# A gated mix of linear attention and an MLP block: column sums moved from TensorE to VectorE, a mask built on GpSimd, and the first loads re-ordered

## The chip, the cores and the metric

The kernel runs on one core of a Trainium2 chip. The metric is device time in microseconds (us), from fourteen runs of the program; beside it stands one execution taken with the profiler. All times below are us from the start of that execution's span unless marked ns. TensorE (PE) multiplies matrices, VectorE (DVE) and ScalarE (ACT) do elementwise work, GpSimd (POOL) does small arithmetic and masks, and SyncE (SP) issues most transfers. Each engine runs its own instructions in order and waits on semaphores for the others.

## The reference

The input x has 2048 rows (tokens) and 640 columns. The output is g * a + (1 - g) * b with a gate g per token.

```
g  = sigmoid((x * gate_w).sum(-1))
# a: linear attention, 32 heads of 20
q, k, v = x @ wqkv                      # 3 x [2048, 640]
phi(t)  = where(t > 0, t + 1, exp(t)) + 1e-6
kv  = sum_s phi(k)[s, d] * v[s, e]      # per head, 20 x 20
z   = sum_s phi(k)[s, d]                # per head, 20: column sums over all tokens
o   = (phi(q) @ kv) / (phi(q) @ z + 1e-6)
a   = o @ wo
# b: mixer block
h   = gelu(layernorm(x) @ w1);  hs = four column groups of h shifted by 1, -1, 2, -2 tokens
x1  = x + hs @ w2
b   = x1 + gelu(layernorm(x1) @ w3) @ w4
```

## The kernel before, in words

Tokens are cut into 16 chunks of 128 (index c), columns into 5 blocks of 128 (index dc). The whole program is written out by hand in one order per engine; PSUM is four buffers of 128 x 1024 float32 that `alloc` and `release` pass round in turn. A matmul needs its contraction along partitions, so x is held twice: as it is (`x_sb`) and transposed (`xT`).

*Start (lines 159 to 342).* Weights of K and the first three x chunks are loaded. Five matmuls on zeros (L308) keep TensorE busy until they arrive. TensorE turns chunks 0 to 2 itself (`x_tr`, L320), and VectorE and ScalarE copy the result out of PSUM (L321, L322). All later chunks of `xT` come by transposing DMAs (L157) that `late_loads` issues on SyncE, with the plain x loads (L154) in between, and then all further weights. A memset of one column of xT (L327), which VectorE does after the copy of chunk 0, holds that list back: the first transposing DMA writes over the same column and has to wait for it. GpSimd builds `mask4`, a 0/1 matrix of which columns belong to which head. TensorE transposes it (L313) and ScalarE copies the result to `E4` (L314), the expansion matrix which spreads a value per head over 4 partitions.

*K stage (L345).* For each chunk: ten matmuls (L252) make k in PSUM; ScalarE takes exp (L244), VectorE makes phi from it (L247, L248) and stores it in `pk`. A G step (L261) follows: x.T @ phi(k), accumulated over chunks.

*Q stage (L383).* Ten Q tiles of 128 x 1024 (L390), each followed by five or six G steps, and by its own phi on ScalarE and VectorE. In between, VectorE does LayerNorm (`ln1_apply`, L226), whose result SyncE transposes by DMA into `lnxT` (L228). After the third tile `z_rows` (L359) sums phi(k) over all tokens on TensorE: 32 matmuls against a matrix of ones (L364), the four chunks of a group in the four column strips, so that each sum comes out 32 times over. ScalarE copies it (L366), VectorE splits it into two bf16 parts (L368, L369). After the fifth tile `z_cols` (L371) adds the strips and turns the sums into columns by ten one-column matmuls (L376, L377) against 1/32; VectorE makes `Zb`, the sums masked by head (L378, L381).

*W1 stage (L495).* A `w1_unit` is ten matmuls (L423), then gelu on ScalarE (L428, L431). Between these units stand the small steps of attention: `den_unit` (the denominators, L470), `rec_piece` (their reciprocals in four pieces, L477), `kv_unit` (L443), six `m_unit`s (L457, the product of kv and wo), `m_move` (through DRAM and back, L462), `rexp_unit` (E4 spreads the reciprocals, L484) and `scale_q` (L493). The order of these calls is the order on each engine. SyncE's loads of W3 (L514) and W4 (L527 to L530) come after `m_move` in the same queue.

*The rest.* W2 (L556) with the residual add (L558) and second LayerNorm, then W3 (L571), the attention output (L597), W4 (L638) and the stores (L609).

Of the kernel before, what the change touches and what calls it, by code (L numbers as in the profile page):

```python
# [8 lines left out]
ACT = mybir.ActivationFunctionType  # L9
# [7 lines left out]
def kernel(  # L17
# [14 lines left out]
    P = 128  # L32
# [20 lines left out]
    def sb(name, cols, dt=BF16):  # L53
        return const.tile([P, cols], dt, name=name)
# [46 lines left out]
    kvT = sb("kvT", 6 * GW)[:].rearrange("p (g d) -> p g d", g=6)  # L101
    warm = sb("warm", 512)
    ident = sb("ident", P)
    ones32 = sb("ones32", 32)
    c32 = sb("c32", 1)
    mask4 = sb("mask4", P)
    mask32 = mask4[:, 0:32]
    E4 = sb("E4", P)
    bmask = sb("bmask", GW, F32)
    g5 = sb("g5", P)  # L110
# [26 lines left out]
    def alloc():  # L137
        return free.pop(0)

    def release(i):  # L140
        free.append(i)
# [11 lines left out]
    def load_x(c0, c1):  # L153
        sp.dma_start(x_sb[:, c0:c1, :], xv[:, c0:c1, :])  # L154

    def load_xT(c0, c1):
        sp.dma_start_transpose(xT[:, :, c0 * P:c1 * P], x2[c0 * P:c1 * P, :])  # L157
# [8 lines left out]
    for dc in range(3):  # L166
# [4 lines left out]
    sp.dma_start(wkg[:, 3:5, 0:D], A_wqkv[3 * P:5 * P, D:2 * D].rearrange("(j p) d -> p j d", p=P))  # L171


    nc.gpsimd.memset(mask4[:], 1.0)
    m4 = mask4[:].rearrange("p (f h) -> p f h", f=4)
    nc.gpsimd.affine_select(out=m4, in_=m4, compare_op=ALU.is_ge, fill=0.0, base=0,
                            pattern=[[0, 4], [-4, 32]], channel_multiplier=1)
    nc.gpsimd.affine_select(out=m4, in_=m4, compare_op=ALU.is_ge, fill=0.0, base=3,
                            pattern=[[0, 4], [4, 32]], channel_multiplier=-1)
    for dc in range(DC):  # L180
        nc.gpsimd.memset(wkg[:, dc, D + 1:D + 2], 1.0)
    nc.gpsimd.memset(ones32[:], 1.0)
    nc.gpsimd.memset(c32[:], 1.0 / 32)
    nc.gpsimd.memset(nhalf[:], -0.5)
    nc.gpsimd.memset(bmask[:], 1.0)
    bm3 = bmask[:].rearrange("p (h e) -> p h e", e=DH)
# [1 line left out]
                            pattern=[[-DH, 6], [0, DH]], channel_multiplier=1)  # L188
    nc.gpsimd.affine_select(out=bm3, in_=bm3, compare_op=ALU.is_ge, fill=0.0, base=DH - 1,
                            pattern=[[DH, 6], [0, DH]], channel_multiplier=-1)  # L190
    nc.gpsimd.memset(hsT[:, :, 0:4], 0.0)
    nc.gpsimd.memset(hsT[:, :, S:S + 4], 0.0)

# [39 lines left out]
    def pop(q, n=1):  # L233
        for _ in range(n):
            if q:
                q.pop(0)()
# [13 lines left out]
    def k_mm(c, p, dc):  # L250
        for (n0, n1) in ((0, 512), (512, KW)):
            mm(PP[p][:, n0:n1], lhsT=xT[:, dc, c * P:(c + 1) * P], rhs=wkg[:, dc, n0:n1],  # L252
               start=(dc == 0), stop=(dc == DC - 1))
# [21 lines left out]
            g_post(i, gp[0])  # L275

    def late_loads():
        load_xT(3, 4)
        load_xT(4, 5)
        load_x(3, 4)  # L280
        load_xT(5, 6)
        load_xT(6, 7)
        load_x(4, 6)
        load_xT(7, 8)
        load_xT(8, 10)
        load_x(6, 9)
        load_xT(10, 11)
        load_xT(11, 13)
        load_x(9, 12)
        load_xT(13, 16)  # L290
        load_x(12, 16)
        rows = lambda w, a, b: w[:, a:b].rearrange("(j p) d -> p j d", p=P)
        sp.dma_start(wq, rows(A_wqkv, 0, D))
        sp.dma_start(w1, rows(B_w1, 0, D))
        sp.dma_start(wv, rows(A_wqkv, 2 * D, 3 * D))
        sp.dma_start(wo6[0:GW, 0:5, :], A_wo[0:5 * GW, :].rearrange("(g r) d -> r g d", r=GW))
        sp.dma_start(wo6[0:gsz[5], 5, :], A_wo[5 * GW:D, :])
        sp.dma_start(w2[:, 0:4, :], B_w2.rearrange("(g c) d -> c g d", c=CG)[0:P])
        for g in range(4):
            sp.dma_start(w2[32 * g:32 * (g + 1), 4, :], B_w2[CG * g + P:CG * (g + 1), :])  # L300
        w1g = w1.rearrange("p k (g c) -> p k g c", c=CG)
        w1x4 = w1x.rearrange("p k (g c) -> p k g c", g=4)
        for g in range(4):
            nc.gpsimd.tensor_copy(w1x4[:, :, g, :], w1g[:, :, g, P:CG])


    for _ in range(5):
        mm(PP[3][:, 512:1024], lhsT=warm[:, 0:P], rhs=warm[:], start=True, stop=True)  # L308
    tg = PP[0][:, 512:1024].bitcast(BF16)
    nc.tensor.transpose(tg[:, 0:DC], g5[0:DC, :], ident[0:DC, 0:DC])  # L310
    for dc in range(DC):
        nc.vector.tensor_copy(wkg[:, dc, D:D + 1], tg[:, dc:dc + 1])
    nc.tensor.transpose(PP[1][:, 0:64].bitcast(BF16), mask4[:], ident[:])  # L313
    act(E4[:], PP[1][:, 0:64].bitcast(BF16), ACT.Copy)  # L314

    def x_tr(c, a, b):
        ta, tb = PP[a][:, 0:512].bitcast(BF16), PP[b][:, 0:512].bitcast(BF16)
        for dc in range(DC):
            t, k = (ta, dc) if dc < 3 else (tb, dc - 3)
            nc.tensor.transpose(t[:, k * P:(k + 1) * P], x_sb[:, c, dc * P:(dc + 1) * P], ident[:])  # L320
        nc.vector.tensor_copy(xT[:, 0:3, c * P:(c + 1) * P], ta[:, 0:3 * P].rearrange("p (j s) -> p j s", j=3))  # L321
        act(xT[:, 3:5, c * P:(c + 1) * P], tb[:, 0:2 * P].rearrange("p (j s) -> p j s", j=2), ACT.Copy)  # L322
# [1 line left out]
    for _ in range(3):  # L324
        alloc()
    x_tr(0, 3, 2)
    nc.vector.memset(xT[:, 0, 3 * P:3 * P + 1], 0.0)  # L327
    late_loads()
    x_tr(1, 1, 2)
    k_mm(0, 0, 0)  # L330
    k_mm(0, 0, 1)
    x_tr(2, 3, 2)
    k_mm(1, 1, 0)
    k_mm(1, 1, 1)
    k_mm(2, 2, 0)
    k_mm(2, 2, 1)
# [19 lines left out]
    gq = [(0, c) for c in range(NCH - 3, NCH)] + [(i, c) for i in range(1, DC) for c in range(NCH)]  # L356
    wqp = wq.rearrange("p k (q j) -> p k j q", j=DC)

    def z_rows():  # L359
        p = alloc()  # L360
        for (n0, n1) in COLS:
            for cc in range(0, NCH, 4):
                for q in range(4):
                    mm(PP[p][32 * q:32 * (q + 1), n0:n1], lhsT=ones32[:], rhs=pk[:, cc + q, n0:n1],  # L364
                       start=(cc == 0), stop=(cc == NCH - 4), tile_position=(0, 32 * q), skip_group_check=True)
        act(zsb[:], PP[p][:, 0:D], ACT.Copy)  # L366
        release(p)
        nc.vector.tensor_copy(zhi[:], zsb[:])  # L368
        nc.vector.tensor_tensor(zlo[:], zsb[:], zhi[:], op=ALU.subtract)  # L369

    def z_cols():  # L371
        p = alloc()
        zh = zhi[:].rearrange("p (q j) -> p j q", j=DC)
        zl = zlo[:].rearrange("p (q j) -> p j q", j=DC)
        for j in range(DC):
            mm(PP[p][:, j:j + 1], lhsT=zh[:, j], rhs=c32[:], start=True, stop=False)  # L376
            mm(PP[p][:, j:j + 1], lhsT=zl[:, j], rhs=c32[:], start=False, stop=True)  # L377
        nc.vector.tensor_copy(zT[:], PP[p][:, 0:DC])  # L378
        release(p)
        for j in range(DC):  # L380
            nc.vector.tensor_scalar(Zb[:, j, :], mask32, zT[:, j:j + 1], None, op0=ALU.mult)  # L381

    n_ = 0  # L383
    for half in range(2):
        for j in range(DC):
            p = alloc()
            for dc in range(DC):
                for tt in range(2):
                    t0 = half * 1024 + tt * 512
                    mm(PP[p][:, tt * 512:(tt + 1) * 512], lhsT=wqp[:, dc, j], rhs=xT[:, dc, t0:t0 + 512],  # L390
                       start=(dc == 0), stop=(dc == DC - 1))
            phi(pqT[:, j, half * 1024:(half + 1) * 1024], PP[p][:], 1024)
            release(p)
            pop(ln1_s)
            if n_ in (1, 2, 3, 4, 7, 8):
                pop(ln1_a, 2)
            for _ in range(6 if n_ == 0 else 5):
                g_unit(*gq.pop(0))
            if n_ == 2:
                z_rows()  # L400
            if n_ == 4:
                z_cols()
            n_ += 1
    while gq:
        g_unit(*gq.pop(0))
    assert not ln1_s
    pop(ln1_a, 4)
    assert not ln1_a

# [56 lines left out]
    def den_unit():  # L466
        p = alloc()
        for j in range(DC):
            for t in range(4):
                mm(PP[p][32 * t:32 * (t + 1), 0:512], lhsT=Zb[:, j, :], rhs=pqT[:, j, t * 512:(t + 1) * 512],  # L470
                   start=(j == 0), stop=(j == DC - 1), tile_position=(0, 32 * t), skip_group_check=True)
        nc.vector.tensor_scalar(den[:], PP[p][:, 0:512], 1e-6, None, op0=ALU.add)
        release(p)

    def rec_piece(k):
        with nc.allow_low_precision(reason="bf16 operand of a product"):
            nc.vector.reciprocal(rden[:, k * P:(k + 1) * P], den[:, k * P:(k + 1) * P])  # L477
# [15 lines left out]
        nc.vector.tensor_tensor(pqT[:, j, s_], pqT[:, j, s_], rexp[:, s_], op=ALU.mult)  # L493

    w1_unit(0, 4)  # L495
    den_unit()
    rec_piece(0)
    w1_unit(0, 0)
    kv_unit()
    rec_piece(1)  # L500
    w1_unit(0, 1)
    m_unit(0)
    m_unit(1)
    rec_piece(2)
    w1_unit(0, 2)
    m_unit(2)
    m_unit(3)
    rec_piece(3)
    w1_unit(0, 3)
    m_unit(4)  # L510
    m_unit(5)
    m_move()
    for dc in range(DC):
        sp.dma_start(w3[:, dc, :], B_w3[dc * P:(dc + 1) * P, :])  # L514
    w1_unit(1, 4)
    w1_unit(1, 0)
    rexp_unit()
    w1_unit(1, 1)
    scale_q(0, 0)
    scale_q(1, 0)  # L520
    scale_q(2, 0)
    w1_unit(1, 2)
    scale_q(3, 0)
    scale_q(4, 0)
    w1_unit(1, 3)
    w4v = B_w4[0:NF * P, :].rearrange("(f p) d -> p f d", p=P)
    sp.dma_start(w4[0:FT, NF, :], B_w4[NF * P:F, :])  # L527
    sp.dma_start(w4[FT:2 * FT, NF, :], B_w4[NF * P:F, :])
# [159 lines left out]
```

## Time and profile before

| what | us |
|---|---|
| median of 14 runs (lowest to highest) | 267.26 (266.93 to 267.86) |
| the profiled execution: its time / its span | 267.64 / 265.9 |
| TensorE busy | 261.6 (98% of the span) |
| VectorE / ScalarE / GpSimd busy | 116.0 / 110.7 / 32.1 |
| K stage from the first turned chunk to the first Q tile | 3.7 to 31.9 |
| Q stage, W1 stage, W2 stage begin at | 31.9, 73.4, 100.1 |

TensorE's busy share is an upper figure, since matmuls are pipelined and their ends are modelled. The chain of work that ended last tells which engine each moment of the span hung on. A bracket at the end of a timeline row is the idle time of that engine before the instruction, and what ended it. Idle time of an engine that nobody waits for costs nothing.

### The profile page before, as it was taken

The numbers are of one execution on the slowest core, as the hardware profiler recorded it, in microseconds if no ns is written. First come the engines' busy times: TensorE is split into PE (matmuls) and PEld (weight loads), VectorE is DVE, ScalarE is ACT, GpSimd is POOL, SyncE is SP. The second block draws the span as 40 slices with busy tenths as digits, with TensorE's granted clock in tenths as the row PEclk, the third lists the DMA queues.
The fourth block names the chain that finished last, engine by engine and source line by source line (L and its number), as shares of the span: only waits on it lengthen the run. The fifth ranks groups of instructions, "written<-read, shape, count | busy, mean of one in ns | idle before, by whom it ended". The sixth has DMA issues, their size and how long they took to land.

```text
span 265.9 us, 4225 instructions
## 1 busy us (share of the span) xinstructions
PE 261.6 (98%) x1698; PEld 136.2 (51%) x1698; DVE 116.0 (44%) x212; ACT 110.7 (42%) x165; POOL 32.1 (12%) x110
## 2 busy tenths in 40 slices
PE   8999999999999999999999999999999999999995
PEld 4555555555545445554444455555544444555552
DVE  2487747665665165999920033233200002233232
ACT  3466664565355671234977522022034444022020
POOL 3000052020200000536770000000000000000000
PEclk9999999999999999999999999999999999999999
DMA  6799995431440269932752001001000000001001
GB/s 213 160 188 248 368 234 123 54 74 25 84 91 0 67 220 357 306 81 49 101 100 49 0 2 49 27 25 49 27 25 0 0 2 0 25 27 49 27 25 49
DMA packets 42207, 23.95 MB, mean 90 GB/s; under 512 B 31052, under 2 KB 41420, under 8 KB 42188
## 3 DMA queue, kind: packets, MB, share of 16 engines
q1 hardware_dynamic: 41602, 23.16, 36.1%
q10 hardware_dynamic: 586, 0.53, 0.6%
q8 instruction: 13, 0.21, 0.3%
q14 instruction: 6, 0.05, 0.1%
HBM read 12.86 MB, written 3.44 MB: 61 GB/s over the span
## 4 chain that ended last, share of the span: by engine, by line
PE 98%; DVE 1%; ACT 0%; issue 0%
PE pp L638 20%; PE pp L571 19%; PE pp L252 8%; PE pp L423 8%; PE pp L597 8%; PE pp L390 8%; PE pp L556 8%; PE pp L261 8%; PE pp L580 2%; PE pp L623 1%; PE pp L632 1%; PE pp L587 1%; PE pp L308 1%; PE pp L457 1%; PE pp L443 1%; PE pp L320 1%
## 5 line engine op out<-in xcount | busy, mean ns | idle before, releaser
L638 PE MATMUL pp<-RB,RXH 128*128 128x512 bf16 (+1 forms) x390 | 54.4, 299 | 0.0
L571 PE MATMUL pp<-lnxT,RA 128*128 128x512 bf16 x240 | 52.1, 379 | 0.0
L638 PEld LDWEIGHTS <-RXH 128*128 128x128 bf16 x390 | 29.7, 98 | 24.2 <-issue 2.1
L571 PEld LDWEIGHTS <-RA 128*128 128x128 bf16 x240 | 23.4, 98 | 28.1
L600 ACT ACTIVATE RXH<-pp,g_all 128x640 f32<-128x640 f32 x16 | 12.7, 794 | 54.9 <-PE pp L597 54.9
L573 ACT ACTIVATE RXH<-pp 128x1024 bf16<-128x1024 f32 x24 | 24.3, 1020 | 26.7 <-PE pp L571 26.7
L244 ACT ACTIVATE eb<-pp 128x640 bf16<-128x640 f32 (+1 forms) x26 | 21.4, 828 | 25.3 <-PE pp L390 16.3
L261 PE MATMUL pp<-RPK,RXH 128*128 128x512 bf16 (+1 forms) x160 | 25.2, 299 | 0.0
L252 PE MATMUL pp<-RA,RXT 128*128 128x512 bf16 (+1 forms) x160 | 24.5, 305 | 0.0
L390 PE MATMUL pp<-RXT,RA 128*128 128x512 bf16 x100 | 23.3, 379 | 0.0
L597 PE MATMUL pp<-Mp,pqT 128*128 128x512 bf16 (+1 forms) x160 | 23.1, 299 | 0.0
L602 DVE SCALAR_TENSOR_TENSOR RPK<-RPK,omg,RXH 128x640 f32<-128x640 f32 x8 | 7.1, 885 | 36.5 <-ACT RXH L600 36.5
L556 PE MATMUL pp<-w,RXH 128*128 128x512 bf16 (+1 forms) x160 | 21.9, 299 | 0.0
L423 PE MATMUL pp<-lnxT,RB 128*128 128x512 bf16 x80 | 18.3, 379 | 0.0
L261 PEld LDWEIGHTS <-RXH 128*128 128x128 bf16 x160 | 12.7, 98 | 10.4
L247 DVE TENSOR_SCALAR eb<-eb 128x640 bf16<-128x640 bf16 (+1 forms) x26 | 9.5, 364 | 19.5 <-ACT eb L244 19.5
L602 DVE SCALAR_TENSOR_TENSOR RXT<-RXT,omg,RXH 128x640 f32<-128x640 f32 x8 | 7.1, 885 | 24.6 <-ACT RXH L600 24.6
L252 PEld LDWEIGHTS <-RXT 128*128 128x128 bf16 x160 | 12.7, 100 | 9.6 <-issue 0.5
L597 PEld LDWEIGHTS <-pqT 128*128 128x128 bf16 x160 | 12.2, 98 | 10.0 <-issue 0.8
L556 PEld LDWEIGHTS <-RXH 128*128 128x128 bf16 x160 | 12.3, 98 | 9.6
L607 DVE SCALAR_TENSOR_TENSOR RXH<-pp,omg,RXT 128x640 bf16<-128x640 f32 x8 | 7.1, 884 | 19.8 <-PE pp L638 19.8
L390 PEld LDWEIGHTS <-RA 128*128 128x128 bf16 x100 | 11.1, 118 | 8.9
(109 smaller groups left out, 237.7 us busy)
## 6 DMA issues: line engine op xcount, KB each, us to landing
out_dram<-RXH SPq DMA_DIRECT2D x15, 160.0 KB, 1.8
RA<-in_B_w_dram SPq DMA_DIRECT2D x5, 432.0 KB, 6.6
RA<-in_A_wqkv_dram SPq DMA_DIRECT2D x2, 800.0 KB, 7.0
RB<-in_B_w_dram SPq DMA_DIRECT2D x1, 1120.0 KB
RXH<-in_A_x_dram SPq DMA_DIRECT2D x2, 480.0 KB, 5.2
RB<-in_B_w_dram SPq DMA_DIRECT2D x1, 960.0 KB, 12.8
RB<-in_B_w_dram SPq DMA_DIRECT2D x1, 800.0 KB, 8.7
Mp<-Mscr SPq DMA_DIRECT2D x1, 800.0 KB
```

The lines of the kernel that those rows point to most:

```text
L244: act(e[:, 0:n], src, ACT.Exp)
L252: mm(PP[p][:, n0:n1], lhsT=xT[:, dc, c * P:(c + 1) * P], rhs=wkg[:, dc, n0:n1], start=(dc == 0), stop=(dc == DC - 1))
L261: mm(PP[p][:, n0:n1], lhsT=x_sb[:, c, i * P:(i + 1) * P], rhs=pk[:, c, n0:n1], start=(c == 0), stop=(c == NCH - 1))
L390: mm(PP[p][:, tt * 512:(tt + 1) * 512], lhsT=wqp[:, dc, j], rhs=xT[:, dc, t0:t0 + 512], start=(dc == 0), stop=(dc == DC - 1))
L423: mm(PP[p][:, tt * 512:(tt + 1) * 512], lhsT=lh, rhs=lnxT[:, dc, t0:t0 + 512], start=(dc == 0), stop=(dc == DC - 1))
L556: mm(PP[p][:, n0:n1], lhsT=hsT[:, fc, 2 + c * P:2 + (c + 1) * P], rhs=w2[:, fc, n0:n1], start=(fc == 0), stop=(fc == DC - 1))
L571: mm(PP[p][:, k * 512:(k + 1) * 512], lhsT=w3[:, dc, (fc + k) * P:(fc + k + 1) * P], rhs=lnxT[:, dc, t * 512:(t + 1) * 512], start=(dc == ...
L573: act(h2T[:, t % 2, fc:fc + 2, :], PP[p][:].rearrange("p (k s) -> p k s", k=2), ACT.Gelu_apprx_tanh)
L597: mm(PP[p][:, n0:n1], lhsT=pqT[:, j, c * P:(c + 1) * P], rhs=Mp[:, j, n0:n1], start=(j == 0), stop=(j == DC - 1))
L600: act(ga, PP[p][:, 0:D], ACT.Copy, scale=g_all[:, c:c + 1])
L602: nc.vector.scalar_tensor_tensor(x1(c), x1(c), omg[:, c:c + 1], ga, op0=ALU.mult, op1=ALU.add)
L638: mm(PP[p][:, n0:n1], lhsT=h2T[:, k, fc, cc], rhs=w4[:, fc, n0:n1], start=False, stop=(fc == NF - 1))
```

## The change

1. `mask4` and its transposition go. `mask32` (32 columns) is built alone, and `E4` directly on GpSimd, by two selects for each of four groups of 32 partitions.
2. `z_rows` goes. In the Q stage VectorE adds up phi(k) of the 16 chunks in float32, fifteen adds of 128 x 640, one or two after each Q tile; the split into two bf16 parts follows after the stage. This leaves 128 partial sums per column, one for each partition, and `z_cols` adds them by the same ten matmuls, now against 1.
3. `z_cols` moves from the fifth Q tile to the W1 stage, and den, the reciprocals, M and their move go one W1 unit further back.
4. There are six matmuls on zeros instead of five.
5. The hold now lies after the copy of the third chunk, and the order of the first K matmuls changes a little. The transposing DMAs follow one another on SyncE; the plain x loads are issued by GpSimd, held by a memset of their own.

```diff
+    nc.gpsimd.memset(E4[:], 1.0)
+    for f in range(4):
+        e4 = E4[32 * f:32 * (f + 1), :]
+        nc.gpsimd.affine_select(out=e4, in_=e4, compare_op=ALU.is_ge, fill=0.0, base=0,
+                                pattern=[[1, P]], channel_multiplier=-4)
+        nc.gpsimd.affine_select(out=e4, in_=e4, compare_op=ALU.is_ge, fill=0.0, base=3,
+                                pattern=[[-1, P]], channel_multiplier=4)
...
     def late_loads():
-        load_xT(3, 4)
-        load_xT(4, 5)
-        load_x(3, 4)
...
-        load_xT(13, 16)
-        load_x(12, 16)
+        for (c0, c1) in ((3, 4), (4, 5), (5, 6), (6, 7), (7, 8), (8, 10), (10, 11), (11, 13), (13, 16)):
+            load_xT(c0, c1)
+        for (c0, c1) in ((3, 4), (4, 6), (6, 9), (9, 12), (12, 16)):
+            nc.gpsimd.dma_start(x_sb[:, c0:c1, :], xv[:, c0:c1, :])
...
-    for _ in range(5):
+    for _ in range(6):
         mm(PP[3][:, 512:1024], lhsT=warm[:, 0:P], rhs=warm[:], start=True, stop=True)
...
-    nc.tensor.transpose(PP[1][:, 0:64].bitcast(BF16), mask4[:], ident[:])
-    act(E4[:], PP[1][:, 0:64].bitcast(BF16), ACT.Copy)
...
     x_tr(0, 3, 2)
-    nc.vector.memset(xT[:, 0, 3 * P:3 * P + 1], 0.0)
-    late_loads()
     x_tr(1, 1, 2)
     k_mm(0, 0, 0)
+    k_mm(1, 1, 0)
+    x_tr(2, 3, 2)
+    nc.vector.memset(xT[:, 0, 3 * P:3 * P + 1], 0.0)
+    nc.vector.memset(x_sb[:, 3, 0:1], 0.0)
+    late_loads()
     k_mm(0, 0, 1)
-    x_tr(2, 3, 2)
-    k_mm(1, 1, 0)
     k_mm(1, 1, 1)
...
-    def z_rows():
...
+    def z_add(c):
+        nc.vector.tensor_tensor(zsb[:], pk[:, 0, :] if c == 1 else zsb[:], pk[:, c, :], op=ALU.add)
+
+    def z_sum():
         nc.vector.tensor_copy(zhi[:], zsb[:])
         nc.vector.tensor_tensor(zlo[:], zsb[:], zhi[:], op=ALU.subtract)
...
-            if n_ == 2:
-                z_rows()
-            if n_ == 4:
-                z_cols()
+            pop(za, 2 if n_ in (5, 6, 9) else 1)
...
+    pop(za, 2)
+    z_sum()
...
     w1_unit(0, 4)
+    w1_unit(0, 0)
+    z_cols()
+    kv_unit()
+    w1_unit(0, 1)
     den_unit()
     rec_piece(0)
-    w1_unit(0, 0)
-    kv_unit()
-    rec_piece(1)
-    w1_unit(0, 1)
+    w1_unit(0, 2)
     m_unit(0)
     m_unit(1)
...
+    w1_unit(1, 4)
     m_unit(4)
     m_unit(5)
+    rec_piece(3)
     m_move()
     for dc in range(DC):
         sp.dma_start(w3[:, dc, :], B_w3[dc * P:(dc + 1) * P, :])
-    w1_unit(1, 4)
     w1_unit(1, 0)
+    w1_unit(1, 1)
     rexp_unit()
-    w1_unit(1, 1)
+    w1_unit(1, 2)
     scale_q(0, 0)
     scale_q(1, 0)
     scale_q(2, 0)
-    w1_unit(1, 2)
+    w1_unit(1, 3)
     scale_q(3, 0)
     scale_q(4, 0)
-    w1_unit(1, 3)
```

## The prediction

> **What bounds the kernel now.** The page comes first, its fourth part (the chain that ended last).
>
> ```profile
> ## 4 chain that ended last, share of the span: by engine, by line
> PE 98%; DVE 1%; ACT 0%; issue 0%
> ```
>
> TensorE sets the time from end to end, and every stage is a stretch of matmuls. So the second view is the same chain in order of time, around the piece that goes away (start, duration, what).
>
> ```profile
> 39.22 2.16 PE pp L390 x10
> 41.38 1.36 PE pp L261 x10
> 42.74 1.20 PE pp L364 x32
> 43.94 2.29 PE pp L390 x10
> 46.22 1.36 PE pp L261 x10
> 47.58 2.16 PE pp L390 x10
> ```
>
> The L390 groups (Q tiles) start 3.52 apart wherever only G units follow (2.16 + 1.36). Around L364, the column sums, the two distances are 4.72 and 3.64, together 1.32 more than 2 x 3.52. So those 32 small matmuls cost 1.20 themselves and 0.12 in changing shape.
>
> The third view is the timeline of VectorE in the same stage. The last bracket is its idle time before an instruction.
>
> ```profile
> 45.38 0.83 DVE L369 TENSOR_TENSOR zlo<-zsb,zhi 128x640 bf16<-128x640 f32 x1
> 50.83 0.43 DVE L247 TENSOR_SCALAR eb<-eb 128x1024 bf16<-128x1024 bf16 x1 [1.05 <-ACT eb L244]
> 58.26 0.43 DVE L247 TENSOR_SCALAR eb<-eb 128x1024 bf16<-128x1024 bf16 x1 [1.76 <-ACT eb L244]
> ```
>
> L369 is the nearest relative of the new adds, and the brackets are the room for them: 1.05 after a tile with two LayerNorm applies, 1.76 after one without.
>
> The fourth view is the start: SyncE's queue, the landing times of the transposed x chunks (L157), and windows with the DMA share in the next to last column.
>
> ```profile
> 4.66 2.60 SPq L157 DMA_TRANSPOSE RXT<-in_A_x_dram  x2
> 7.31 0.58 SPq L154 DMA_DIRECT2D RXH<-in_A_x_dram  x1
> 7.93 2.52 SPq L157 DMA_TRANSPOSE RXT<-in_A_x_dram  x2
> ```
> ```profile
> DMA to landing us min/median/max: 3.2/4.1/5.2
> ```
> ```profile
> 7.00:10.40 3.40, 3.40 (x27) 1.94 (x26) 0.24 (x2) 1.21 (x4) 0.00 (x0) 1.00 0.73 144
> 10.40:31.90 21.50, 21.50 (x159) 12.17 (x158) 16.42 (x30) 14.77 (x41) 0.00 (x0) 1.00 1.07 250
> ```
> ```profile
> 6.66 7.96 PE L252 MATMUL pp<-RA,RXT 128*128 128x512 bf16 x56
> ```
>
> The last row fixes deadlines: a chunk of K takes ten matmuls, 1.36, and chunks 3, 4 and 5 are the last thirty of this run, which ends for the next instruction at 14.46. So chunk 3 is needed at 10.37, chunk 4 at 11.73, chunk 5 at 13.09. By the same reading chunk 8 is needed at 18.68, chunk 13 at 26.85. After 10.4 the DMA engines are full.
>
> **What the Trainium skill says.** (1) "VectorE: DVE Perf Modes", section "Mode 2×_2P", has a float32 tensor_tensor at one element per cycle: 640 elements at 0.96 GHz are 0.67 and a fixed part. The 0.83 of L369 agrees. (2) "DMA: Bandwidth & Descriptors", section "Queues, rings and completion order", has each DMA engine go round robin between queues, a packet at a time. Before, nearly all late transfers sit in SyncE's one queue, so no run here shows it; it matters below. (3) "SBUF — State Buffer", section "SBUF: two separate sides", says that a DMA issued from GpSimd has its descriptors written by GpSimd, which VectorE locks out during two-port operations. Not shown here; L247 holds at most 0.33 at a time in the K stage. (4) "TensorE: Matmul & The Clock Gate", Part 1, has the matmuls at half clock until some microseconds of activity. The trace agrees: L308 runs at 626 ns against 379 later, and the short spacing begins near 7.0.
>
> **The change, part by part.**
>
> Column sums leave TensorE: 32 L364 matmuls, -1.32 as above. ScalarE loses the 0.71 copy of L366, which nobody waited for.
>
> VectorE gains 15 adds of 128x640. Price 0.83 each (L369); bounds 0.67 from the skill and 0.89 from L602, which also writes float32. One add in a hole of 1.05 and two (1.66) in holes of 1.76 fit; the others are 2.03 after the first tile, 1.04 after the third once the casts and 1.32 of matmuls are gone, and 1.05 after the fifth once L378/L381 and z_cols have left. So 0 on the path. At 0.89 two adds overrun by 0.02. Behind a late L247 would wait L248, which frees a PSUM buffer; with three buffers for Q tiles that is needed two tiles, some 4 us, later. Cover gone, the price is the overrun alone.
>
> After the loop VectorE has 2 adds of the last tile, 2 more, and the casts (0.49 + 0.83): 4.64 after the last L248, which ended at 70.57, now 1.71 earlier (1.32 and 0.39, next item): 68.86 + 4.64 = 73.5. The four last applies follow, until 75.1. Their transposes (1.3 apart on SyncE, 2.6 to landing before) arrive by about 81.5; w1_unit(1, 4), the first reader, comes at 87.
>
> z_cols moves behind the second W1 unit. It cost 3.88 + 3.55 - 2 x 3.52 = 0.39 and costs that again: 0. There TensorE arrives at 73.42 - 1.71 + 4.32 = 76.0; its operand is ready at 73.5.
>
> den moves behind kv and W1 (0, 1): TensorE reaches it at 76.0 + 0.39 + 1.69 + 2.16 = 80.3. Before it VectorE has the applies (75.1), the gate (0.6), the four copies of W1 (0, 4) (1.72), zT and Zb (0.16 + 0.78): 78.5. Slack 1.8, so 0. M, m_move and behind it on SyncE the W3 and W4 loads come about one W1 unit (2.2) later, less the 1.3 gained. W3 was issued at 95.95 to 98.85 and landed in 6.6, for use at 122; Mp is read at 151. All 0. rec_piece(3) ends near 93, the expansion comes at 94.2; scale_q then ends at 99.4, before the first residual add at 100.4. Each is 0, and about 1 of slack is what is left.
>
> Expansion matrix on GpSimd: one TensorE transpose (0.11 at half clock) and a ScalarE copy go. GpSimd gets eight selects at 0.32 (L176) and small ones, so it is busy until about 6.1 instead of 3.6. Its x loads wait for a memset until 7.4 anyway: 0. Behind them on GpSimd are the w1x copies and the LayerNorm arithmetic, from 32.98 on before; x of chunk 3 is first read at about 16.5.
>
> Warm-up: a sixth 512-column matmul adds 0.43 at half clock. Against the transpose and the wait for ScalarE's copy (L314) that leaves the third x turning 0.24 later at half clock, about 0.12 once the clock doubles: +0.12.
>
> The hold: the transposes waited for a memset at 4.56 and were issued at 4.66. The memset now follows the third PSUM copy (L321, 6.69 to 7.05, now 7.30), so xT of chunk 3 is issued at 7.45, 2.8 later. SyncE then issues transposes without x loads in between, 1.27 each: 8.72, 9.99. Deadlines 10.49, 11.85, 13.21. With the shortest landing of before, 3.2, they arrive at 10.65, 11.92, 13.19: late by 0.16 once. With the median, 4.1 (which had queues in front of it), 1.06. I take 0.3, as the queue in front is gone but five x loads now run beside: +0.3. A stall once is not paid twice, since 1.27 is under 1.36. What is late next is chunk 8, in a two-chunk transfer.
>
> x loads in GpSimd's queue: 13 chunks of 164 KB. A window of transposes alone (13 to 15) moves 194 GB/s, 0.84 per chunk; one of plain loads (26 to 31) 373, 0.44. From about 8.0 the total is 13 x (0.84 + 0.44) = 16.6, done near 25: in time for chunk 13 if shared kindly. Wq, 800 KB or 2.1 more, lands near 28 for 31.9. I take 0 beyond the stall above; the other end is a rival.
>
> Sum: -1.32 + 0.12 + 0.3 = -0.90. The profiled execution had a span of 265.9 and took 267.64; its change is 265.0 and 266.7. The median of the runs is 267.26, so 266.4.
>
> **The rivals.** *Slower: the x loads starve the transposes.* The price is in the packets: the 45 transposed chunks of 164 KB make up most of the page's 31,052 packets under 512 B, so they go in pieces of about 256 B, 640 a chunk, 40 per engine, at 0.021 each (194 GB/s over 16 engines); an x row is 1,280 B, 0.055 (373 GB/s). If the engines take turns packet by packet (2), a transposed chunk takes 40 x 0.076 = 3.0 instead of 1.27 for the 104 x rows per engine, some 8 us. Chunks 4 and 5 are then each late by 3.0 - 1.36 = 1.65. Net 3.3 + 0.12 - 1.32 = +2.1: 269.4. It decides from a total stall of 1.2 on. For it: the DMA share of 1.07 leaves no reserve. Against it: the share is 0.73 just where the first chunks move, and packets may be larger than pieces.
>
> *No change: the start gives it back.* Landing stays at 4.1 (stall 1.06), or chunk 8 or 13 is late by about 1. Net -0.2, 267.1.
>
> *VectorE becomes the bound.* Adds at 1.1 instead of 0.83, or GpSimd's small operations blocked by them, make the last applies, zT and Zb late by over 1.8 and TensorE waits at den, or at the expansion. With a stall of 1.0 there: 267.4. Against it is the row of L369; the Q stage's VectorE load only goes from 25.35 of 41.5 to about 34 of 39.8.
>
> That the change doesn't do what it says, because TensorE idles where L364 was, is this last case.
>
> **How the numbers follow.** Forecast 0.48, starvation 0.30, start gives it back 0.16, VectorE 0.06. A measurement tells 0.2%, 0.53 us, from no change. The forecast case lies from 265.9 (-1.32: no stall, nothing lost in the warm-up) to 266.7 (a stall of 0.6): faster 0.48. The two middle cases are mostly within the bound: same 0.22. Starvation: slower 0.30. The range reaches from 265.8, 0.1 below the forecast case for the measurement, to 269.4; the worse half of the starvation case is left out.
>
> **What would show it.** Right: no L364 row; L390 starts 3.52 apart through the Q stage; L247's brackets near 0.2; K stage chunks 1.36 apart with one gap under 0.5 before chunk 3; den straight behind L423. Wrong: L252 groups with waits on a transposed x chunk, landings of L157 over 4.5, or a TensorE wait before L470 or L484.

## The result and the profile after

The changed kernel takes 277.0 us (median of 10 runs, 276.2 to 278.3) against 267.4 for the kernel before (48 runs): 1.036 times as long, interval 1.0335 to 1.0379. It is 3.6% slower, 9.6 us; the prediction was 266.4, in a range that ended at 269.4.

The profiled execution has a span of 275.68 against 265.94, 9.74 more. The start of the first Q tile divides it:

| | before | after | difference |
|---|---|---|---|
| first Q tile | 31.75 | 42.98 | +11.23 |
| from there to the end | 234.19 | 232.70 | -1.49 |
| span | 265.94 | 275.68 | +9.74 |

```profile
31.75 2.32 PE L390 MATMUL pp<-RXT,RA 128*128 128x512 bf16 x10
42.98 2.32 PE L379 MATMUL pp<-RXT,RA 128*128 128x512 bf16 x10
```

(L379 is L390 of before.) So the part that was meant to gain did gain, and the K stage before it lost seven to eight times as much. The page's fourth part, the chain that ended last, now has DMA in it:

```profile
## 4 chain that ended last, share of the span: by engine, by line
PE 92%; DMA 5%; SPq 1%; DVE 1%; issue 0%; ACT 0%
```

Where that is, TensorE's timeline of the K stage shows (start, duration; idle time before it and its releaser in the bracket). L255 is L252 of before; each row is one chunk.

```profile
10.57 1.52 PE L255 MATMUL pp<-RA,RXT 128*128 128x512 bf16 x10 [0.33 <-DVE eb L250]
14.19 1.53 PE L255 MATMUL pp<-RA,RXT 128*128 128x512 bf16 x10 [2.09 <-DMA RXT<-in_A_x_dram]
22.66 2.86 PE L255 MATMUL pp<-RA,RXT 128*128 128x512 bf16 x10 [6.94 <-DMA RXT<-in_A_x_dram]
26.37 1.53 PE L255 MATMUL pp<-RA,RXT 128*128 128x512 bf16 x10
```

Chunk 3 starts at 10.57, against 10.37 before; its bracket is a wait for VectorE, not for x. Chunk 4 waits 2.09 for its transposed x and chunk 5 waits 6.94, together 9.03. Then chunk 5 takes 2.86, not 1.52: TensorE has lost its clock. The chain in order of time gives that part a price (start, duration, what):

```profile
6.96 1.30 SPq L155
...
9.61 13.01 DMA RXT<-in_A_x_dram
22.66 2.86 PE pp L255 x10
25.52 1.01 PE pp L264 x4
26.53 1.36 PE pp L255 x10
```

At full clock the ten and the four matmuls take 1.36 and 0.54, here 2.86 and 1.01: 1.97 lost. The sum is 0.20 + 9.03 + 1.97 = 11.20 of the 11.23. The same rows show the culprit: the load of chunk 5 was issued at 9.61 and landed 13.01 later. The landing times of the transposed chunks, SyncE's queue and the windows of the K stage (length; busy time of PE, PEld, DVE, ACT, POOL; granted clock; DMA share; GB/s) go with it:

```profile
DMA to landing us min/median/max: 4.7/5.8/13.0
```
```profile
6.95 21.30 SPq L155 DMA_TRANSPOSE RXT<-in_A_x_dram  x9
28.29 0.58 SPq L286 DMA_DIRECT2D RA<-in_A_wqkv_dram  x1
```
```profile
10.50:15.00 4.50, 2.33 (x16) 1.21 (x17) 3.99 (x7) 1.55 (x6) 0.59 (x1) 1.00 1.07 283
15.00:19.00 4.00, 0.72 (x6) 0.27 (x4) 1.17 (x3) 1.48 (x4) 0.00 (x0) 1.00 1.21 156
19.00:22.60 3.60, 0.00 (x0) 0.00 (x0) 0.00 (x0) 0.00 (x0) 0.00 (x0) 0.57 1.08 127
22.60:26.40 3.80, 3.74 (x15) 1.81 (x16) 0.11 (x1) 0.77 (x2) 0.00 (x0) 0.51 1.00 196
```

The median landing went from 4.1 to 5.8 and the longest from 5.2 to 13.0. The DMA share is 1 or more in all four windows, and until 15 the engines move more bytes than before (283 GB/s against 176 in the same window, and 250 over the K stage), but many of them are plain rows that are needed much later. After 15 the rate falls to 156 and 127. The granted clock falls to half in the third window, about 3.8 us after TensorE went idle at 15.72, and stays there until 26.3, 3.7 after the matmuls start again. The Trainium skill says so ("TensorE: Matmul & The Clock Gate", Part 1: throttled after an idle window of about 3.4 us, released by as much activity), and the trace agrees: the wait of 2.09 left the clock alone, the one of 6.94 did not. SyncE was held up too: its nine transposes took until 28.25 to issue, one of them 6.88 alone, and the load of wq behind them came at 28.29 and landed at 34.89.

The rest of the kernel is as predicted. In the chain of the Q stage no L364 is left and the tiles stand 3.52 apart:

```profile
50.45 2.16 PE pp L379 x10
52.61 1.36 PE pp L264 x10
53.97 2.16 PE pp L379 x10
56.12 1.36 PE pp L264 x10
```

VectorE takes the new adds (L352) at 0.82 and still waits 0.3 for ScalarE behind them:

```profile
55.38 0.79 DVE L229 TENSOR_SCALAR lnxs<-RXH,me,rs 128x640 bf16<-128x640 bf16 x2
56.09 0.82 DVE L352 TENSOR_TENSOR zsb<-zsb,RPK 128x640 f32<-128x640 f32 x1
57.22 0.43 DVE L250 TENSOR_SCALAR eb<-eb 128x1024 bf16<-128x1024 bf16 x1 [0.31 <-ACT eb L247]
```

And den (L459) stands straight behind W1; its operand Zb was done at 88.64 + 0.78 = 89.42, 2.1 before it is needed:

```profile
88.64 0.78 DVE L370 TENSOR_SCALAR Zb<-mask,zT 128x32 bf16<-128x32 bf16 x5
```
```profile
87.61 1.65 PE pp L432 x30
89.26 2.27 PE pp L412 x10
91.52 1.19 PE pp L459 x20
92.72 2.26 PE pp L412 x10
```

### The profile page after: what moved, and what is told of

Its sections match the earlier page's. It is cut to its first block, busy times and chain, and to the rows that moved or that the text cites. A ratio compares the mean times of both kernels' runs of the same rounds, so it can differ in the third digit from the quotient of the medians.

```text
span 275.7 us, 4188 instructions
## 1 busy us (share of the span) xinstructions
PE 262.0 (95%) x1666; PEld 135.6 (49%) x1666; DVE 127.7 (46%) x228; ACT 109.8 (40%) x163; POOL 38.9 (14%) x123
## 4 chain that ended last, share of the span: by engine, by line
PE 92%; DMA 5%; SPq 1%; DVE 1%; issue 0%; ACT 0%
PE pp L628 20%; PE pp L561 19%; PE pp L264 8%; PE pp L412 8%; PE pp L587 8%; PE pp L546 8%; PE pp L379 8%; PE pp L255 6%; DMA RXT<-in_A_x_dram 5%; PE pp L570 2%; PE pp L613 1%; PE pp L622 1%; PE pp L301 1%; SPq L155 1%; PE pp L577 1%; PE pp L446 1%
## 5 line engine op out<-in xcount | busy, mean ns | idle before, releaser
L561 PEld LDWEIGHTS <-RA 128*128 128x128 bf16 x240 | 23.4, 98 | 28.1
L255 PE MATMUL pp<-RA,RXT 128*128 128x512 bf16 (+1 forms) x160 | 25.9, 312 | 9.4 <-DMA RXT<-in_A_x_dram 9.0
L379 PE MATMUL pp<-RXT,RA 128*128 128x512 bf16 x100 | 23.2, 379 | 0.0
L255 PEld LDWEIGHTS <-RXT 128*128 128x128 bf16 x160 | 12.9, 102 | 20.2 <-DMA RXT<-in_A_x_dram 9.7
L597 DVE SCALAR_TENSOR_TENSOR RXH<-pp,omg,RPK 128x640 bf16<-128x640 f32 (+2 forms) x9 | 7.3, 810 | 19.1 <-PE pp L628 17.2
```

Of the source, the lines that this page charges most:

```text
L561: mm(PP[p][:, k * 512:(k + 1) * 512], lhsT=w3[:, dc, (fc + k) * P:(fc + k + 1) * P], rhs=lnxT[:, dc, t * 512:(t + 1) * 512], start=(dc == ...
L597: nc.vector.scalar_tensor_tensor(oc[:, n0:n1], PP[p][:, n0:n1], omg[:, c:c + 1], x1(c)[:, n0:n1], op0=ALU.mult, op1=ALU.add)
```

## The experiments

Two edits of the start can be the cause: the hold after the third turned chunk, and the x loads in GpSimd's queue. Theory A: the 13 chunks of plain x, given to a second queue at once, take the DMA engines from the transposes. Theory B: the hold issues the transposes too late, and the queue matters little. Theory C: loading from GpSimd is slow or harmful by itself, whatever its amount. The quoted expectations use these letters, with the numbers that each gives. Each median is compared with runs of the kernel before on the same chip; since chips differ by some tenths of a us, the ratio says more than the time.

**e1, x loads back on SyncE; the late hold stays.**

```diff
...
-            nc.gpsimd.dma_start(x_sb[:, c0:c1, :], xv[:, c0:c1, :])
+        load_xT(3, 4)
+        load_xT(4, 5)
+        load_x(3, 4)
+        load_xT(5, 6)
...
```

> The changed kernel, with the plain x loads back on SyncE between the transposes as before; the late hold stays. Theory A (the x loads on a second queue take the DMA engines from the transposes): TensorE's wait for the transposed x falls from 9.0 us to 0.3 to 1.1, time 266.2 to 267.1. Theory B (the hold alone makes the transposes late): the wait stays over 5, time over 272.

Measured: 268.23 (12 runs), ratio 1.0007 (0.9977 to 1.0037). 8.8 of the 9.6 are gone with the queue alone (9.4 by the two ratios). B falls. But it is 1 us above what A gave, and TensorE still waits in the K stage. The waits of its profile (total, times, longest):

```profile
PE pp L321 <- DMA RXH<-in_A_x_dram: 0.7, 1, 0.7
PE pp L255 <- DMA RXT<-in_A_x_dram: 0.6, 1, 0.6
```

The 0.6 is chunk 8, the first of a two-chunk transfer; the 0.7 is the third chunk of plain x, which landed late in this execution, and a hold that depends on it passes the delay on to every transpose.

**e2, the early hold; x stays on GpSimd.** The three lines of the hold go back behind the first turned chunk.

> The changed kernel, with the hold back after the first turned chunk; the x loads stay on GpSimd. Theory A: one or two more chunks get through before the x loads start, the wait is still 6 to 9, time 273 to 277. Theory B: the wait is gone, time about 266.

Measured: four runs, 269.12, 275.38, 276.21 and 277.87, median 275.79 against 267.52. Two lie in A's range and one 0.9 above it. The profile is of the one that ended at 269.12: its one wait for a transposed chunk is 2.0, with no loss of clock seen behind it. The other three have a mean granted clock of 0.981 to 0.988 on record, as the changed kernel has (0.980 to 0.988), so they lost the clock as it did. Four runs that scatter so widely don't settle it; e7 below makes the same test in the old kernel, and there most of the loss stays.

**e3, the start of before: x on SyncE and the early hold; all other edits stay.**

> The changed kernel, with both put back: x loads on SyncE and the early hold; column sums on VectorE, the mask on GpSimd, the W1 order and the sixth matmul on zeros stay. Both theories: no wait in the K stage, minus 1.32 for the column sums, plus 0.1 for the sixth matmul, time 265.9 to 266.2. If VectorE's adds cost something after all: 266.5 or more, with a wait of TensorE in the Q or W1 stage.

Measured: 266.09 (20 runs), ratio 0.9942 (0.9915 to 0.9969), and again as e11, on another occasion:

> The kernel with both start edits put back once more, for a narrower interval: ratio to before 0.994 to 0.996.

Measured: 267.25 (22 runs), ratio 0.9968 (0.9944 to 0.9992). The second is a little above the 0.994 to 0.996 that was expected; both intervals lie below 1. From the first Q tile to the end they take 232.87 and 232.86, so the gain of 1.3 of the Q stage is kept, and their K stage has no wait for a transposed chunk. The chain of e3's page:

```profile
PE 98%; DVE 1%; ACT 0%; issue 0%
```

This version is faster than both kernels.

**e4, x loads issued by ScalarE.**

```diff
-            nc.gpsimd.dma_start(x_sb[:, c0:c1, :], xv[:, c0:c1, :])
+            aq.dma_start(x_sb[:, c0:c1, :], xv[:, c0:c1, :])
```

> The changed kernel, with the plain x loads issued by ScalarE instead of GpSimd, everything else equal: again a second queue, whose packets in the profile are one row of 1,280 B and not 5,120 B as in GpSimd's queue. Theory A with turns by packet: a chunk of transposes takes about 3.0 instead of 1.27 while x lasts, wait 2.5 to 4.5, time 268.5 to 270.5. Theory A with turns that don't depend on the packet: as with GpSimd, 275 to 277. Theory C (only GpSimd's way of writing descriptors is slow): wait under 1.1, time under 267.2.

Measured: 276.74 (4 runs), ratio 1.0319 (1.0261 to 1.0377). The loss is as large without GpSimd, but a second thing went wrong. Its waits:

```profile
PE pp L255 <- DVE RPK L251: 5.1, 1, 5.1
PE pp L255 <- DMA RXT<-in_A_x_dram: 2.2, 1, 2.2
```

ScalarE, the issuer, stood for 10.0 at its own loads (7.90 to 17.9) with the K stage's exponentials behind them; so TensorE waited 5.1 for phi and 2.2 for x. It is not the issuing that takes so long: each issue is 0.33 to 0.50. The fourth load starts at 10.62, 0.02 after the first has landed (10.60), and the fifth 0.02 after the transposed chunk 5; each of the two waits for the semaphore of that earlier load, which it uses again. The chain shows the second case (start, duration):

```profile
10.51 7.00 DMA RXT<-in_A_x_dram
17.51 0.02 issue
17.53 0.37 ACTq L284
```

The records of the transfers do tell something. From GpSimd x goes in records of 5,120 B, four rows each; from ScalarE in records of one row, 1,280 B. Between 10 and 17 the kernel before moved 514 rows beside 2,827 transposed pieces of 256 B, the changed kernel 1,160 rows (290 records) beside 1,086 pieces. Over the whole time in which x waited in the second queue, from 8.9 to 16.5, e4 moved about 1,150 rows beside 1,875 pieces. So from either queue, and in records of either size, x took far more of the engines than its place in one queue had given it. The packet-turn figure of 268.5 to 270.5 missed on time, but ScalarE's own standing is in that time.

**e5, only x of chunks 3 to 5 on GpSimd, the rest on SyncE; late hold.**

> The changed kernel, with only the x loads of chunks 3, 4 and 5 on GpSimd (3 chunks in the second queue instead of 13); the others are back on SyncE between the transposes, the late hold stays. Theory A with one x row per 256 B piece of a transposed chunk: 24 rows per DMA engine instead of 104, the transposes lose 24 x 0.055 = 1.3 us once, time 0 to 1.3 above the kernel with all x loads on SyncE and the same hold: 268.2 to 269.5. Theory C (a GpSimd load as such slows the transposes, however little it moves): 275 or more.

Measured: 267.52 (20 runs), ratio 0.9999 (0.9979 to 1.0018). C falls in its plain form: the same queue with three chunks in place of thirteen harms nothing. A's range began at 268.2 and was missed by 0.7; by the ratios e5 (0.9999) and e1 (1.0007) are level, and an added cost is not seen.

**e6, the kernel before with the late hold alone.** The memset and the call of the late loads move behind the third `x_tr`.

> The kernel before, with only the hold moved behind the third turned chunk. If the hold costs about 2 us by itself, as the run with x on SyncE suggests: 269 to 270. If that came from something else in that kernel: 267.3 to 268.

Measured: 269.48 (4 runs), ratio 1.0077 (1.0050 to 1.0105): the hold costs 2.1 by itself. Its waits are 1.3 for a transposed chunk (chunk 7) and 0.6 for the plain x that the turning reads:

```profile
PE pp L252 <- DMA RXT<-in_A_x_dram: 1.3, 1, 1.3
...
PE pp L320 <- DMA RXH<-in_A_x_dram: 0.6, 1, 0.6
```

**e7, the kernel before with x on GpSimd alone, early hold.**

> The kernel before, with only the plain x loads moved to GpSimd's queue, early hold. Theory A: as with the early hold in the changed kernel, 6 to 9 slower than before and scattered, 270 to 278. Theory B (it takes the late hold as well): within 1 of before.

Measured: 275.92 (4 runs), ratio 1.0271 (1.0200 to 1.0343). One edit in the old kernel brings 7 to 8 us. Its landing times and wait stand beside those of the changed kernel (4.7/5.8/13.0, 9.0):

```profile
DMA to landing us min/median/max: 4.4/6.3/11.2
```
```profile
PE pp L252 <- DMA RXT<-in_A_x_dram: 4.9, 2, 4.8
```

**e8, as e3 but with the hold after the second turned chunk.**

> The kernel with both start edits put back, but the hold behind the second turned chunk instead of the first. If each 0.9 that the hold is later makes the transposes late by as much once their slack of about 1.5 is used: no cost yet, 265.9 to 266.4. If the cost grows with the hold from the start: about 267.

Measured: 266.48 (20 runs), ratio 0.9934 (0.9903 to 0.9965), as good as e3. There was room for one step of the hold and none for two.

**e9, as e3 but all x on GpSimd, in small portions:** chunks 3 to 5 at the start, the others each held by phi of a chunk three to six earlier. Four small copies on GpSimd also come later.

```diff
+    def pool_x(c0, c1):
+        nc.vector.memset(x_sb[:, c0, 0:1], 0.0)
+        nc.gpsimd.dma_start(x_sb[:, c0:c1, :], xv[:, c0:c1, :])
...
+        if c in (3, 6, 9):
+            pool_x(*{3: (6, 9), 6: (9, 12), 9: (12, 16)}[c])
```

> The kernel with both start edits put back, but with the x loads in GpSimd's queue one after another: chunks 3 to 5 with the hold (after the first turned chunk), the next three loads each held behind the phi of chunks 3, 6 and 9; the transposes follow one another on SyncE. Nothing else changes but the place of four small copies on GpSimd. Theory A (what hurts is a backlog of x rows that takes turns with the transposes): little or no wait, 266 to 267.5. Theory C (loads from GpSimd beside transposes are slow as such): over 271.

Measured: 267.05 (20 runs), ratio 0.9952 (0.9926 to 0.9978). The same bytes through the same queue, and the transposes land within 5.1:

```profile
DMA to landing us min/median/max: 3.7/4.5/5.1
```

So it is the backlog in the second queue, not the use of the queue. This is the clearest of the runs.

**e10, late hold, x on SyncE, the first five transposes ahead of every x load.**

> The changed kernel with all x loads on SyncE and the late hold, but the five single-chunk transposes ahead of the first two x loads. If the late hold cost 2.1 because SyncE then also spends 0.6 on each x load between the transposes: 267.3 to 267.8, as with three chunks on GpSimd. If the cost is the late issue alone: 268.0 to 268.5, as with x between.

Measured: 268.32 (20 runs), ratio 1.0008 (0.9984 to 1.0032), as e1. If x in front of the transposes were what makes the late hold cost, this order would have won it back. The late issue alone costs it; chunk 8 waits 0.6 as in e1.

After these, the size was still open: packet turns gave 3.3 of stall, the changed kernel has 9.03. Four more runs keep the late hold and vary what waits in the second queue.

**e12, nine chunks in four loads from ScalarE** (so that it need not stand for a fifth); x of chunks 12 to 15 goes on SyncE behind the transposes.

```diff
-        for (c0, c1) in ((3, 4), (4, 6), (6, 9), (9, 12), (12, 16)):
-            nc.gpsimd.dma_start(x_sb[:, c0:c1, :], xv[:, c0:c1, :])
+        for (c0, c1) in ((3, 4), (4, 6), (6, 9), (9, 12)):
+            aq.dma_start(x_sb[:, c0:c1, :], xv[:, c0:c1, :])
+        load_x(12, 16)
```

> The changed kernel with x of chunks 3 to 11 issued by ScalarE in four loads (1.5 MB of backlog) and x of chunks 12 to 15 by SyncE behind the transposes; late hold. ScalarE should then not stand at a fifth issue (it stood there for 10.0 us with five). If the backlog costs the same from any queue, transposed chunks are late by 5 us or more in all, the rate falls under 160 GB/s somewhere between 15 and 22, and the time is 273 to 277. If turn-taking is all that a backlog on ScalarE's queue brings, and the crawl belongs to GpSimd's queue, the wait for transposed x stays near the 2.2 us seen with five loads and the time is 268.5 to 271.

**e13, the same from GpSimd.**

> The same with GpSimd as issuer of the four loads. The changed kernel gave 277.0 with five loads, three chunks on GpSimd gave 267.5. If the crawl comes with a backlog in GpSimd's queue: 273 to 277, with a wait of 5 us or more for transposed x and a half clock behind it. If it needs the whole of 2.1 MB, or if four loads are below a limit: 268 to 271, as the ScalarE version.

Measured: e12 270.19 (6 runs), ratio 1.0099 (1.0066 to 1.0132); e13 270.56 (6 runs), ratio 1.0118 (1.0091 to 1.0146). The intervals overlap: at this amount no difference between the issuers is seen. In both, the chain runs through the transposed load of chunk 5 (e12, then e13; start, duration):

```profile
9.29 6.61 DMA RXT<-in_A_x_dram
9.31 6.97 DMA RXT<-in_A_x_dram
```

TensorE's timeline of e13 is close to what the slower rival described:

```profile
10.34 1.52 PE L255 MATMUL pp<-RA,RXT 128*128 128x512 bf16 x10 [0.39 <-DMA RXT<-in_A_x_dram]
13.61 1.54 PE L255 MATMUL pp<-RA,RXT 128*128 128x512 bf16 x10 [1.75 <-DMA RXT<-in_A_x_dram]
16.33 1.54 PE L255 MATMUL pp<-RA,RXT 128*128 128x512 bf16 x10 [1.18 <-DMA RXT<-in_A_x_dram]
```

Three chunks in a row are late, 3.3 in all, chunk 4 by 1.75 where the rival has 1.65, and the clock stays full. In e12 TensorE's waits are split otherwise, 2.1 for phi, since ScalarE stood for 3.0 at its loads, and 0.7 for x.

**e14, all thirteen chunks from GpSimd in four loads** (2, 3, 4 and 4 chunks), and **e15, nine chunks in five loads** (1, 2, 2, 2 and 2).

> The changed kernel with all 13 chunks of plain x on GpSimd (2.1 MB) in four loads instead of five (2, 3, 4, 4 chunks); late hold. With nine chunks in four loads the time was 270.6. If the amount of the backlog makes the collapse: 274 to 278, a wait of 5 us or more for transposed x and a half clock behind it. If it is the fifth load outstanding, whatever its size: 269.5 to 272, with waits of 3 to 4 us and no half clock.

> Nine chunks of plain x on GpSimd (1.5 MB) in five loads instead of four, chunks 12 to 15 on SyncE behind the transposes; late hold. If the amount makes the collapse: as the nine chunks in four loads, 269.5 to 272. If it is the fifth load outstanding: 274 to 278.

Measured: e14 280.98 (4 runs), ratio 1.0493 (1.0405 to 1.0582), above both of its ranges; e15 274.50 (4 runs), ratio 1.0214 (1.0135 to 1.0293). The thirteen chunks bring the collapse in four loads too, so the fifth load is not its condition; but nine chunks in five loads cost 3.9 more than in four (2.6 by the ratios; no run of e13 is over 271.2, none of e15 under 273.5), so the amount alone doesn't set it either. Both simple answers fall. The rate falls in both: two windows each of e14 and e15, and one of the kernel before (columns as above):

```profile
13.00:15.00 2.00, 0.11 (x2) 0.00 (x0) 1.73 (x5) 0.77 (x2) 0.00 (x0) 1.00 1.23 106
15.00:17.00 2.00, 0.00 (x0) 0.00 (x0) 0.64 (x1) 0.00 (x0) 0.00 (x0) 0.80 0.93 77
```
```profile
15.00:17.00 2.00, 1.54 (x10) 0.73 (x10) 0.77 (x1) 0.41 (x1) 0.00 (x0) 1.00 1.47 193
17.00:19.00 2.00, 0.00 (x0) 0.00 (x0) 1.15 (x2) 1.07 (x4) 0.00 (x0) 1.00 0.97 64
```
```profile
19.00:21.00 2.00, 2.00 (x17) 1.13 (x15) 1.18 (x3) 1.13 (x5) 0.00 (x0) 1.00 1.26 64
```

e13 keeps 234 and 195 GB/s in the same two windows as e15's. But the last row, and e13's 105 from 20 to 22, say that a short fall of the rate is no mark of this collapse: TensorE works through it where no chunk is due. In the changed kernel the rate is 104 from 17 to 21, while chunk 5 is due.

The landing times in the traces show that the two queues do not take turns row by row. In the changed kernel the transposed chunks 3, 4 and 5 land at 10.44, 14.14 and 22.62, and the first, third and last load of plain x at 10.23, 14.70 and 22.78. In e7, e13, e14 and e15, too, each of these three chunks lands within 0.6 of the first, the third and the last plain load; in e2 chunks 4, 5 and 6 do so, and from ScalarE (e4, e12) chunks 3, 4 and 5 land within 0.6 of the second, third and fourth. Between 13 and 14 the changed kernel moved 53 records of x and no transposed piece, although the load of chunk 5 had been issued at 9.61. So a transposed chunk came in together with a whole plain load, with up to thirteen chunks of x before chunk 5. What sets these turns no run shows.

## Why the prediction was wrong

*Column sums, -1.32:* right. From the first Q tile to the end the changed kernel and the versions that keep this part gain 1.05 to 1.49; e6 and e7, which lack it, 0.03 and 0.17.

*VectorE's adds at 0.83, den, z_cols, the W1 units, the mask, each 0:* right. The adds took 0.82, den's slack was 2.1 against 1.8 worked out, no engine wait of TensorE appears after the K stage. The VectorE rival is refuted by that.

*Warm-up, +0.12:* not seen. In e3 the third turning is later at first, but chunk 3 starts at 10.27, 0.1 earlier than before. Nothing hangs on it.

*The hold, "I take 0.3":* the step failed in size. It costs 2.1 in the old kernel (e6) and 2.1 between e1 and e3. The issue came at 6.95, sooner than the 7.45 of the prediction, so the start was not the error. The sum looked at the deadline of chunk 3 and took a stall to be paid once; but what became late was chunk 7 or 8, which the prediction names as "what is late next" and gives no price in its sum (only a rival has it, at about 1). And it took the landing of the third plain x chunk, on which the hold now depends, as fixed.

*x loads in GpSimd's queue, "I take 0 beyond the stall above":* this step made the forecast wrong. It costs 8.8 (changed kernel against e1) or 7 to 8 (e7 against before). The working counted bytes, "in time for chunk 13 if shared kindly", and sharing was the question. Before the change each transpose lay in SyncE's queue at its place between x loads, so the order of need was the order of service. With 2.1 MB waiting in a second queue, rows that are needed much later went ahead of transposes that were due. The price in that working was misread as well, though this did not decide: the window of "transposes alone" (13 to 15) also held 72 plain rows, and where pieces moved alone the rate was anything from 142 GB/s (before, 14 to 15) to 291 (e7, 24 to 25), not 194.

*The rival "the start gives it back":* this is what the hold does alone, with x left on SyncE: e1 and e10 come out level with the kernel before, with chunk 8 late, as it says.

*The slower rival:* right that the x loads starve the transposes, and right in size for a smaller backlog. Its way of reckoning is not borne out: it lets the engines alternate between one row and one piece, and over the time in which x waited the eight runs with such a backlog have 0.5 to 1.3 rows to a piece on average, but in the lumps that the landing times show. The Trainium skill has the round robin go by packets ("DMA: Bandwidth & Descriptors", section "Queues, rings and completion order"), without saying how packets of two kinds compare; no run here shows what a packet holds. That e13's waits add up to the rival's 3.3 is therefore in part luck. In the changed kernel two terms are missing from it. One is the fall of the clock, 1.97: in e15 a stall of 2.16 kept the clock and one of 3.74 lost it. The other is that the engines' total rate did not hold: the rival lets x be done after some 8 us, and it took from 9.2 to 22.2, with 127 to 156 GB/s at the end of it though the engines show as full. In e2's profiled execution, the quick one, x was done in 7.8 (9.25 to 17.0) and the stall was 2.0. Against e1, which has the same late hold, nine chunks in four loads cost 2.5 to 3.0 by the ratios (e12, e13) and the changed kernel 9.4; so 6 to 7 come from this collapse and the half clock behind it.

What makes the rate collapse while a chunk is due is open. It was seen in the changed kernel, e7, e14 and e15, all with five loads or thirteen chunks waiting in GpSimd's queue, and not in e13 or in e2's quick execution. Point (3) of the prediction, VectorE locking GpSimd out, is no likely cause: GpSimd had issued its last load by 11.1, and from 19 to 22.6 VectorE did nothing while the rate was 127. e4 doesn't settle whether it needs GpSimd, since its fifth load went out only at 17.5, after chunk 5 had landed. Open too is why the third plain chunk lands about 1 us later in some executions.

## What to carry to other kernels

One queue that holds loads in order of need is a schedule; moving a part of them to a second queue gives that order up, and here loads that were needed late went ahead of transposes that were due. Where a second queue is wanted, give it little at a time, each portion released by work that comes shortly before its use, as in e9. When a hold is moved, price every transfer behind it against its own deadline, and where a stall of TensorE may reach 3 to 4 us (3.74 lost the clock here, 2.16 did not), add the matmuls that then run at half clock.

## What the runs showed of the hardware

- Plain loads in a second queue beside transposes in SyncE's: 1,160 rows of 1,280 B to 1,086 pieces of 256 B between 10 and 17 in the changed kernel, 514 to 2,827 from one queue before. The transposed chunks 3, 4 and 5 landed within 0.6 of the first, third and last plain load in the changed kernel, e7, e13, e14 and e15.
- The issue of a transposing DMA can hold its engine: one took SyncE 6.88 in place of 1.3 and ended at 22.87, 0.25 after chunk 5 landed; in e7 one took 5.64 and ended at 18.61, 0.06 after chunk 5 landed.
- A DMA share near or above 1 went with anything from 64 GB/s (before, 19 to 21) to 283 (the changed kernel, 10.5 to 15). It tells that the engines have work, not that they move data at their rate.
